# A gated linear attention and a gated scan on one core: the alpha copy, the first group's states, the first block and the last store in smaller pieces, and one block in the next turn

## The chip, the cores and the metric

The kernel runs on one core of one Trainium2 chip. The metric is the device time of one execution in microseconds (us). Engines are named TensorE (PE, with its weight loads PEld), VectorE (DVE), ScalarE (ACT), GpSimd (POOL) and SyncE (SP, here a queue that issues transfers).

## What is computed

```python
# B, H, S, D = 4, 8, 768, 48
for t in range(S):
    state = alpha[:, :, t, :, None] * state + einsum('bhd,bhe->bhde', k[:, :, t], v[:, :, t])
    y[:, :, t] = einsum('bhd,bhde->bhe', q[:, :, t], state)
x = y as (B, S, H * D)                       # 384 columns
val, gate = split(x @ w_in)                  # 512 columns each
h[t] = exp(A_log) * h[t - 1] + val[t]        # a scan over S, per column
out = (silu(gate) * h) @ w_out               # 384 columns
```

All arithmetic is in float32; the weights come as 64-bit numbers and are converted on the chip.

## The kernel before

**Tiling.** Each of the 4 sequences is cut into 3 groups of 256 steps, which gives 12 groups, m = 0 to 11. A group has G = 2 chunks of 128 steps and four half chunks of L = 64. The 8 heads lie in two halves of partitions (i = 0, 1), with four heads along the free axis in each.

**Attention of a group m.** Alpha, q and k are brought to a layout with the channels along partitions, either by products with the identity on TensorE and copies by ACT (`turned`, L675, `copy_turned`, L685; a pair of PSUM banks for each tensor; `alphas` and `straighten` do the whole of it) or by a transpose on VectorE (`turn`, L589, in all later groups). Then `scan_P` (L620) forms running products of alpha, `scan_V` (L629) the reversed scan that k is scaled by, with three small operations between the two scans (ratio, L634 or L636, ends, L638, lower, L640). `scaled_k` and `scaled_q` write Zk and Zq. `scores` (L709) multiplies them into two pairs of PSUM banks, one pair for each chunk; `masks` (L722) takes the causal part on VectorE and copies the rest (K, dS) by ACT. `values` and `carried` form the output y of the group, `states` (L769) the half chunks' contributions to the state, which `add_banks` or, for later sequences, `add_up` sum. `first_values`, `first_carried`, `first_states` and `first_join` (L816 to L852) do the same for group 0, with v in the tile `wide` and the summed states in `wide_S`. `join` puts y into xT with transfers.

**Projection of a group n.** `project(n, cc)` (L880), cc = 0 to 3, makes two products of 128 x 256 from three input blocks kk each, a scan over them on VectorE (hh, L894), a silu on ACT (sg, L899); the function that it returns multiplies the two into f (L901), on VectorE for n below 2, else on POOL. `output(n)` (L903) makes two products of 128 x 384 with w_out; ACT copies each out and SP stores it.

**Weights.** `low(i)` (L535, ACT) and `convert(i)` (L541, two operations of VectorE and an addition on POOL) make weight part i; parts 0 to 3 are w_in for cc = 0 to 3, parts 4 and 5 the halves of w_out. `project(0, cc)` needs part cc.

**Order.** The program is scheduled by hand: each engine works off its instructions in the order of the calls. What stands before the loop (L920 to L976) is group 0's attention. Turn n of the loop (L998) holds the projection of group n and the attention of group n + 1; turns 0 and 1 are written out singly, as they still convert weights and straighten groups 1 to 3 on TensorE. PSUM has four banks in a ring (tag "mm") and the fixed banks s0, s1, y0 and y1. `bank_pair("s")` takes the fixed pair. A transfer waits on its queue until the one eight before it has landed.

Of the kernel before, what the change touches and what calls it, by code (L numbers as in the profile page):

```python
# [345 lines left out]
def fast(  # L346
# [143 lines left out]
    def constants():  # L490
# [23 lines left out]
        for n, t in enumerate(Zqs):  # L514
            for i in range(2):
                rows = ds(64 * i, 64)
                nc.gpsimd.tensor_copy(out=t[rows, :, :, 0:D].rearrange("p u h d -> p (u h) d"),
                                      in_=ident[rows, None, ds(64 * i, D)].to_broadcast([64, 8 * G, D]))
            if n == 0:
                load_v(0, nc.gpsimd)  # L520
                nc.gpsimd.memset(tri, 1.0)
                nc.gpsimd.affine_select(out=tri, in_=tri, compare_op=ALU.is_ge, fill=0.0, base=0,
                                        channel_multiplier=-1, pattern=[[1, C]])
                for h in range(2):
                    nc.gpsimd.tensor_copy(out=mask[ds(L * h, L)], in_=tri[ds(L * h, L), ds(L * h, L)])

    def bits_of(i):
# [100 lines left out]

    def scan_V(m, P):  # L629
        al = als[m % 2]  # L630
        g = m % NG
        last = P[:, :, GC]
        if g:
            nc.vector.tensor_mul(ratio[:, m], last, ends[:, :, GC])  # L634
        else:
            nc.vector.tensor_scalar(out=ratio[:, m], in0=last, scalar1=1.0 / FIRST_PRODUCT, scalar2=None,  # L636
                                    op0=ALU.mult)
        nc.vector.reciprocal(ends[:, :, GC], last)  # L638
        if g < NG - 1:
            nc.vector.tensor_copy(out=lower[:, :, 0], in_=last)  # L640
        V = p1.tile([C, 4 * GP], FP32, tag="V", name="V")
        nc.vector.tensor_tensor_scan(out=V[:, ::-1], data0=al[:, 1:4 * GP + 1][:, ::-1],  # L642
                                     data1=ends.rearrange("p h t -> p (h t)")[:, ::-1],
                                     initial=0.0, op0=ALU.mult, op1=ALU.add)
        return by_place(V)

# [27 lines left out]

    def turned(m, name, part, t):  # L675
        raw = steps_of(name, m)
        tp = t.rearrange("p (j x) -> p j x", j=NJ // 2)
        for j in range(NJ // 2):
            for i in range(2):
                nc.tensor.matmul(tp[ds(64 * i, 64), j],  # L680
                                 raw[:, ds(i * ROW + (NJ // 2 * part + j) * D, 64)], ident,
                                 start=True, stop=True, skip_group_check=True)
        return tp.rearrange("p j (c h) -> p h c j", h=4)

    def copy_turned(to, part, tp):  # L685
        nc.scalar.activation(by_runs(to)[:, :, :, ds(NJ // 2 * part, NJ // 2)], tp, AF.Copy)  # L686

    def alphas(m, tag=None):
        to = by_place(als[m % 2])[:, :, 1:GP]
        for part, t in enumerate(bank_pair(tag)):  # L690
            copy_turned(to, part, turned(m, "a", part, t))

    def straighten(m, name):
        to = plain(name)
        for part, t in enumerate(bank_pair()):
            copy_turned(to, part, turned(m, name, part, t))
        return to
# [10 lines left out]

    def scores(m):  # L709
        Zk, Zq = Zks[m], Zqs[m % 2]  # L710
        scs[m] = [bank_pair("s"), bank_pair()]
        for c in range(G):
            for p in range(4):
# [55 lines left out]
    def states(m):  # L769
        first = (m % NG) * 2 * G  # L770
        st = [t[:, 0:G * 4 * D].rearrange("p (c j d) -> p c j d", c=G, j=4) for t in bank_pair("s")]
        n = [G, G - (first + 2 * G == NS)]
        for c in range(G):
            for p in range(4):
                for h in range(2):
                    if c < n[h]:
                        rows = ds(L * h, L)
                        for i in range(2):
                            nc.tensor.matmul(st[h][ds(64 * i, 64), c, p, :], (K0, dS[m % 2][1])[i][rows, c, p, :] if m < NG else Ks[i][rows, c, p, :],  # L779
                                             wide[rows, c, ds(2 * D * (4 * i + p), D)] if m == 0 else  # L780
                                             vs[m % NV][rows, c, 4 * i + p, 0:D],
                                             start=True, stop=True, skip_group_check=True)
# [3 lines left out]
        for h in range(2):  # L786
            nc.scalar.activation(parts[h][:, 0:n[h], :, 0:D], st[h][:, 0:n[h]], AF.Copy)  # L787

# [12 lines left out]
    def add_banks(m, st):  # L801
        for u in range(4):
# [3 lines left out]
            Ss[j] = sums[j % NB]  # L806
            nc.vector.tensor_add(Ss[j][:, :, 0:D], st[u % 2][:, u // 2], Ss[j - 1][:, :, 0:D])

# [21 lines left out]
    def first_carried(us):  # L830
        for u in us:
            for i in range(2):
                rows = ds(64 * i, D)
# [4 lines left out]
    def first_states(st):  # L838
        to = [t.rearrange("p (h d) -> p h d", d=D)[:, ::2, :] for t in wide_S]
        Ss[3] = sums[3]  # L840
        to.append(sums[3][:, :, 0:D])
        nc.scalar.activation(to[0], st[0][:, 0], AF.Copy)
        for u in range(1, 4):
            nc.vector.tensor_add(to[u], st[u % 2][:, u // 2], to[u - 1])

# [33 lines left out]

    def project(n, cc):  # L880
        if cc == 0:
# [6 lines left out]
        pv, pg = [t[:, 0:GC] for t in bank_pair()]  # L888
        for vg, pj in enumerate((pv, pg)):
            for kk in range(NK):  # L890
                nc.tensor.matmul(pj, w_ins[cc][:, kk, vg, :], xT[:, kk, :],  # L891
                                 start=(kk == 0), stop=(kk == NK - 1))
        hh = p2.tile([C, GC], FP32, tag=f"h{cc}", name="hh")
        nc.vector.tensor_tensor_scan(  # L894
            out=hh, data0=a_dec[:, cc:cc + 1].to_broadcast([C, GC]), data1=pv,
            initial=prev_h[cc][:, GC - 1:GC] if n % NG else 0.0, op0=ALU.mult, op1=ALU.add)
        prev_h[cc] = hh
        sg = p2.tile([C, GC], FP32, tag="sg", name="sg")
        nc.scalar.activation(sg, pg, AF.Silu)  # L899
        engine = nc.vector if n < 2 else nc.gpsimd  # L900
        return lambda: engine.tensor_mul(fs[n][cc], sg, hh)  # L901

    def output(n):  # L903
        b, g = divmod(n, NG)
        os = [t[:, 0:DM] for t in bank_pair()]
        def evict(c):
            o_sb = p2.tile([C, DM], FP32, tag="o_sb", name="o_sb")
            nc.scalar.activation(o_sb, os[c], AF.Copy)  # L908
            nc.sync.dma_start(out=out[b, ds(g * GC + c * C, C), :], in_=o_sb)

        for ccs in (range(NI - 1), range(NI - 1, NI)):
            for c in range(G):
# [3 lines left out]
                if ccs.stop == NI:  # L916
                    evict(c)

# [20 lines left out]
    keep_warm(3, 256)  # L939
    alphas(0, "s")  # L940
    tq = straighten(0, "q")
# [9 lines left out]
    P = scan_P(0)  # L951
    V = scan_V(0, P)
    half = turned(1, "k", 0, bank())
    for c in range(G):
        scaled_k(0, tk, V, c)
        scaled_q(0, tq, P, c)
    tk = plain("k")
    copy_turned(tk, 0, half)
    scores(0)
    masks(0)  # L960
    low(0)
    convert(0)
# [35 lines left out]
    for n in range(N):  # L998
        m = n + 1
        if n == 0:  # L1000
            f0 = project(n, 0)
            copy_turned(tk, 1, turned(1, "k", 1, bank()))
            tq = straighten(1, "q")
            V = scan_V(1, P)
            low(2)
            scaled_k(1, tk, V)
            convert(2)
            f1 = project(n, 1)
            low(3)
            scaled_q(1, tq, P)  # L1010
            f0()
            f1()
            alphas(2)
            tk = straighten(2, "k")
            load_raw("k", 3, nc.sync)
            convert(3)
            first(m)
            tq = straighten(2, "q")
            load_raw("q", 3, nc.sync)
            junk(1)  # L1020
            low(4)
            P = scan_P(2)
            f2 = project(n, 2)
            V = scan_V(2, P)
            values(m, True)
            st = states(m)
            add_banks(m, st)
            f3 = project(n, 3)
            third(m)
            load_v(3, nc.sync)  # L1030
            for c in range(G):
                scaled_k(2, tk, V, c)
                scaled_q(2, tq, P, c)
            f2()
            f3()
        elif n == 1:
            scores(m)
            alphas(3)
            load_raw("a", 4, nc.sync)
            convert(4)  # L1040
            masks(m)
            junk(2)
            low(5)
            values(m, True)
            st = states(m)
            P = scan_P(3)
            f0 = project(n, 0)
            add_banks(m, st)
            convert(5)
            f1 = project(n, 1)  # L1050
            f0()
            tk = plain("k")
            turn("k", tk)
            load_raw("k", 4, nc.sync)
            third(m)
            load_v(4, nc.sync)
            f1()
            junk(3)
            V = scan_V(3, P)
            f2 = project(n, 2)  # L1060
            scaled_k(3, tk, V)
            f2()
            output(0)
            f3 = project(n, 3)
            tq = plain("q")
            turn("q", tq)
            scaled_q(3, tq, P)
            f3()
        else:
            first(m)  # L1070
            if n > 1:
                load_raw("q", n + 2, nc.sync)
# [72 lines left out]
```

## Time and profile before

| | us |
|---|---|
| median of 3 runs (lowest, highest) | 288.7 (288.54, 290.04) |
| the profiled execution | 288.26 |
| its span on the core | 286.5 |
| first alpha product on TensorE | 4.57 |
| first P scan on VectorE, from and to | 8.11, 10.41 |
| first scores on TensorE | 14.57 |
| project(0, 0) on TensorE begins | 23.62 |
| project(1, 0) on TensorE begins | 54.05 |
| scores(3) on TensorE begin | 76.69 |
| last copy out on ACT, from and to | 280.17, 280.66 |
| last store landed | 284.33 |

The span is that of the program's instructions on the core. The time of the execution has 1.8 us around it. A row of a timeline has the start, the time taken, the engine, the line, the operation, the tiles (out<-in) with partitions x elements, and how many instructions are merged in it. On TensorE a float32 product counts as two instructions. A row's time includes the drain of the pipeline, so the next row can start before it ends. TensorE's granted clock was full over the span, apart from the tail. The alpha products at 4.57 still went at half the later pace until 5.87 (0.213 us for a pair of rows, then 0.110).

### The profile page before, as it was taken

What the parts mean: (1) busy time and instruction counts of PE and PEld (TensorE: products, weight loads), DVE (VectorE), ACT (ScalarE), POOL (GpSimd) and SP (SyncE); (2) the same over time, 40 slices, a digit from 0 to 9 for tenths busy, and PEclk for the clock granted to TensorE, in tenths of its full rate; (3) what the DMA queues carried; (4) which work ended last, traced back from release to release, by engine and by line L of the source; (5) the groups of instructions that cost most, each with busy time, mean ns of one, the idle gap of its engine ahead of it and who ended that gap; (6) DMA issues with size and microseconds to landing.
All of it is one profiled execution on the core that took longest, in us unless ns stands there. A gap on an engine that the chain in (4) does not pass through costs nothing.

```text
span 286.5 us, 9591 instructions
## 1 busy us (share of the span) xinstructions
PE 276.3 (96%) x4096; PEld 220.2 (77%) x4096; DVE 217.1 (76%) x276; ACT 110.5 (39%) x242; POOL 94.7 (33%) x108
## 2 busy tenths in 40 slices
PE   7889999999999999999999999999999999999991
PEld 6888888886688688788787787787786886886860
DVE  7888999996599499499499498597696795299310
ACT  3765672651335325324333343442451451431111
POOL 8125221420046155142154173142172172241220
PEclk9999999999999999999999999999999999999997
DMA  6999871715691981981972962964944901100101
GB/s 187 345 281 321 249 186 30 185 25 135 170 207 37 228 203 41 235 190 44 256 168 66 261 140 66 268 137 107 250 114 110 239 16 30 59 21 23 55 6 63
DMA packets 51524, 41.22 MB, mean 144 GB/s; under 512 B 27312, under 2 KB 49264, under 8 KB 51472
## 3 DMA queue, kind: packets, MB, share of 16 engines
q1 hardware_dynamic: 50256, 39.37, 52.9%
q8 instruction: 34, 0.56, 0.9%
q10 hardware_dynamic: 960, 0.59, 0.8%
q0 software_dynamic: 256, 0.56, 0.7%
q14 instruction: 18, 0.15, 0.2%
HBM read 32.54 MB, written 4.72 MB: 130 GB/s over the span
## 4 chain that ended last, share of the span: by engine, by line
PE 87%; DVE 7%; DMA 1%; ACT 1%; issue 1%; DVEq 0%; ACTq 0%
PE mm L891 44%; PE mm L914 22%; PE y L752 4%; PE s L779 4%; PE y L765 4%; PE s L718 3%; PE mm L718 3%; PE mm L680 2%; DVE P L625 2%; DVE V L642 2%; DMA raw_a<-in_alpha_dram 1%; PE s L680 1%; PE y L835 1%; DVE Zk L609 1%; PE y L827 1%
## 5 line engine op out<-in xcount | busy, mean ns | idle before, releaser
L891 PE MATMUL mm<-xT,w_in 128*128 128x256 f32 x576 | 133.9, 385 | 0.3 <-ACT xT L849 0.3
L891 PEld LDWEIGHTS mm<-xT,w_in 128*128 128x128 f32 x576 | 106.5, 190 | 17.2 <-issue 0.7
L914 PE MATMUL mm<-w_out,f 128*128 128x384 f32 x176 | 58.6, 486 | 0.0
L914 PEld LDWEIGHTS mm<-w_out,f 128*128 128x128 f32 x176 | 33.4, 190 | 21.0
L899 ACT ACTIVATE sg<-mm 128x256 f32<-128x256 f32 x48 | 18.5, 385 | 76.0 <-PE mm L891 75.8
L901 POOL TENSOR_TENSOR f<-sg,hh 128x256 f32<-128x256 f32 x40 | 30.6, 767 | 45.9 <-ACT sg L899 44.5
L799 POOL TENSOR_TENSOR sum<-sum,dS 128x192 f32<-128x192 f32 x30 | 30.0, 1001 | 19.9 <-ACT dS L787 18.4
L736 POOL TENSOR_TENSOR AK<-AK,mask 128x512 f32<-128x512 f32 x9 | 11.5, 1277 | 68.2 <-ACT AK L734 68.2
L894 DVE TENSOR_TENSOR_SCAN hh<-a_dec,hh,mm 128x256 f32<-128x256 f32 x32 | 23.0, 719 | 14.5 <-PE mm L891 12.3
L908 ACT ACTIVATE o_sb<-mm 128x384 f32<-128x384 f32 x24 | 11.8, 491 | 50.3 <-PE mm L914 50.3
L642 DVE TENSOR_TENSOR_SCAN V<-al,ends 128x1028 f32<-128x1028 f32 x12 | 30.6, 2548 | 0.1
L625 DVE TENSOR_TENSOR_SCAN P<-al,lower 128x1028 f32<-128x1028 f32 x12 | 28.6, 2380 | 2.1 <-ACT al L686 2.0
L733 DVE TENSOR_TENSOR A<-s,mask 128x256 f32<-128x256 f32 x9 | 3.8, 424 | 30.5 <-PE s L718 30.5
L590 DVE STREAM_TRANSPOSE k<-raw_k 128x1024 f32<-128x1024 f32 x9 | 18.3, 2030 | 0.0
L590 DVE STREAM_TRANSPOSE q<-raw_q 128x1024 f32<-128x1024 f32 x9 | 18.2, 2017 | 0.0
L600 DVE TENSOR_TENSOR Zq<-q,P 128x1024 f32<-128x1024 f32 (+1 forms) x14 | 16.3, 1166 | 0.3
L590 DVE STREAM_TRANSPOSE al<-raw_a 128x1024 f32<-128x1024 f32 x8 | 16.3, 2043 | 0.0
L552 POOL TENSOR_TENSOR w_in<-w_in,wr 128x768 int32<-128x768 int32 x4 | 9.1, 2286 | 21.7 <-DVE w_in L550 21.7
L752 PEld LDWEIGHTS y<-AK,v 64*64 64x64 f32 x352 | 12.2, 134 | 3.8 <-issue 3.3
L752 PE MATMUL y<-AK,v 64*64 64x64 f32 x352 | 14.7, 221 | 0.2 <-DVE lower L624 0.2
L609 DVE TENSOR_TENSOR Zk<-k,V 128x1024 f32<-128x1024 f32 (+1 forms) x14 | 14.7, 1050 | 0.2
L752 PE MATMUL y<-A,v 64*64 64x64 f32 x352 | 14.7, 221 | 0.0
(129 smaller groups left out, 362.8 us busy)
## 6 DMA issues: line engine op xcount, KB each, us to landing
out_dram<-o_sb SPq DMA_DIRECT2D x24, 192.0 KB, 3.5
v<-in_v_dram SPq DMA_DIRECT2D x22, 192.0 KB, 3.5
raw_k<-in_k_dram SPq DMA_DIRECT2D x18, 184.0 KB, 4.0
raw_q<-in_q_dram SPq DMA_DIRECT2D x18, 184.0 KB, 3.9
raw_k<-in_k_dram SPq DMA_DIRECT2D x18, 176.0 KB, 4.0
raw_q<-in_q_dram SPq DMA_DIRECT2D x18, 176.0 KB, 4.4
wbits<-in_moe_w_in_dram SPq DMA_DIRECT2D x4, 768.0 KB, 7.9
raw_a<-in_alpha_dram SPq DMA_DIRECT2D x16, 184.0 KB, 4.7
```

Of the source, the lines that this page charges most:

```text
L590: nc.vector.transpose(out=by_runs(to).rearrange("p h c j -> p h j c"), in_=raws[name][:, 0:4 * ROW].rearrange("p (h j d) -> p h j d", h=4, ...
L609: nc.vector.tensor_mul(Zks[m][:, ds(c0, n)].rearrange("p c h t -> p h c t"), t[:, :, at].rearrange("p h (c t) -> p h c t", t=C), V[:, :, 1 ...
L625: nc.vector.tensor_tensor_scan(out=P, data0=al[:, 0:4 * GP], data1=lower.rearrange("p h t -> p (h t)"), initial=0.0, op0=ALU.mult, op1=ALU ...
L642: nc.vector.tensor_tensor_scan(out=V[:, ::-1], data0=al[:, 1:4 * GP + 1][:, ::-1], data1=ends.rearrange("p h t -> p (h t)")[:, ::-1], init ...
L718: nc.tensor.matmul(scs[m][c][i][ds(L * h, L), ds(p * (L + D), L + D)], Zk[rows, c, p, ds(h * L, L)], Zq[rows, u, p], start=True, stop=True ...
L752: nc.tensor.matmul(ys[m][i][ds(64 * s, 64), e, ds(c * C + h * L, L)], v_sb[rows, c, 4 * i + p, :], As[i][rows, c, p, :], start=across and ...
L799: nc.gpsimd.tensor_add(Ss[j][:, :, 0:D], Ss[j - 1][:, :, 0:D], part)
L891: nc.tensor.matmul(pj, w_ins[cc][:, kk, vg, :], xT[:, kk, :], start=(kk == 0), stop=(kk == NK - 1))
L894: nc.vector.tensor_tensor_scan(out=hh, data0=a_dec[:, cc:cc + 1].to_broadcast([C, GC]), data1=pv, initial=prev_h[cc][:, GC - 1:GC] if n % ...
L899: nc.scalar.activation(sg, pg, AF.Silu)
L901: return lambda: engine.tensor_mul(fs[n][cc], sg, hh)
L914: nc.tensor.matmul(os[c], fs[n][cc][:, ds(c * C, C)], w_outs[cc // 2][:, cc % 2, :], start=(cc == 0), stop=(cc == NI - 1))
```

## The change

- Alpha of group 0 goes through four banks (s0, s1, y1, y0) in quarters, with four copies of 256 columns by ACT, where there were two of 512. v of group 0 is loaded by POOL after both Zq tiles and the mask have been made, instead of between the two Zq tiles.
- `scan_V` keeps only what V needs ahead of V. The ratio of a sequence's first group and `lower` come after it (`after_V`), for group 0 after the masks.
- The second half of straighten(1, k) moves from turn 0 to between the two chunks of scores(0).
- `states(0)` uses two pairs of banks, one for each chunk.
- `first_carried` finishes y[0] before y[1], and `project(0, 0)` goes through the input blocks kk in the outer loop.
- In turns 0 and 1 project(0, 3) moves from turn 0 to turn 1, the conversions 2 to 5 and the products f stand elsewhere, and q of group 3 is loaded in the other layout and straightened by TensorE and ACT (`straighten(3, "q")`) instead of turned by VectorE.
- The last store of the program is made in two halves, copied out by ACT and VectorE and stored from ACT's and SP's queues.

```diff
-            if n == 0:
-                load_v(0, nc.gpsimd)
+            if n:
                 nc.gpsimd.memset(tri, 1.0)
...
+                load_v(0, nc.gpsimd)
...
+    def after_V(m, P):
         last = P[:, :, GC]
+        if m % NG == 0:
+            nc.vector.tensor_scalar(out=ratio[:, m], in0=last, scalar1=1.0 / FIRST_PRODUCT, scalar2=None,
+                                    op0=ALU.mult)
+        if m % NG < NG - 1:
+            nc.vector.tensor_copy(out=lower[:, :, 0], in_=last)
...
+    def turn_over(m, name, to, tags=(None, None)):
+        size = NJ // len(tags)
+        for n, tag in enumerate(tags):
+            js = range(size * n, size * (n + 1))
+            copy_turned(to, js, turned(m, name, js, bank(tag)))
...
+        pair = bank_pair("s")
+        pairs = [pair, bank_pair() if m == 0 else pair]
...
     def first_carried(us):
-        for u in us:
-            for i in range(2):
+        for i in range(2):
+            for u in us:
...
+        order = [(vg, kk) for vg in range(2) for kk in range(NK)]
+        if n == 0 and cc == 0:
+            order.sort(key=lambda x: x[1])
...
-                    evict(c)
+                    if n < N - 1 or c == 0:
+                        evict(c)
+                    else:
+                        evict(c, 0, DM // 2, nc.scalar, nc.scalar)
+                        evict(c, DM // 2, DM // 2, nc.vector, nc.sync)
...
-    alphas(0, "s")
+    alphas(0, ("s0", "s1", "y1", "y0"))
...
-    scores(0)
+    copy_turned(tk, halves[0], part)
+    scores(0, [0])
+    copy_turned(tk, halves[1], turned(1, "k", halves[1], bank()))
+    scores(0, [1])
     masks(0)
+    after_V(0, P)
```

Turns 0 and 1 as they stand after the change:

```python
        if n == 0:
            f0 = project(n, 0)
            tq = straighten(1, "q")
            load_steps("q", 3, [nc.sync])
            V = scan_V(1, P)
            low(2)
            f1 = project(n, 1)
            scaled_k(1, tk, V)
            scaled_q(1, tq, P)
            alphas(2)
            tk = straighten(2, "k")
            load_raw("k", 3, nc.sync)
            convert(2)
            first(m)
            tq = straighten(2, "q")
            junk(1)
            low(3)
            P = scan_P(2)
            f0()
            f1()
            values(m, True)
            st = states(m)
            add_banks(m, st)
            h2, f2 = project(n, 2, True)
            V = scan_V(2, P)
            third(m)
            load_v(3, nc.sync)
            for c in range(G):
                scaled_k(2, tk, V, c)
                scaled_q(2, tq, P, c)
                if c == 0:
                    h2()
        elif n == 1:
            scores(m)
            alphas(3)
            load_raw("a", 4, nc.sync)
            low(4)
            masks(m)
            convert(3)
            f2()
            junk(2)
            values(m, True)
            st = states(m)
            add_banks(m, st)
            g0 = project(n, 0)
            P = scan_P(3)
            low(5)
            f3 = project(0, 3)
            convert(4)
            f3()
            g0()
            convert(5)
            g1 = project(n, 1)
            third(m)
            load_v(4, nc.sync)
            tk = plain("k")
            turn("k", tk)
            load_raw("k", 4, nc.sync)
            g1()
            tq = straighten(3, "q")
            load_raw("q", 4, nc.sync)
            junk(3)
            V = scan_V(3, P)
            output(0)
            g2 = project(n, 2)
            scaled_k(3, tk, V)
            scaled_q(3, tq, P)
            g2()
            project(n, 3)()
```

With `late`, `project` returns the scan hh and the product f as two functions, to be called where they are wanted (`h2`, `f2`).

## The prediction

> **What bounds the kernel now.** I read the busy times first, then the chain of waits in order of time, then TensorE's own waits and VectorE's timeline for the first 55 us.
>
> ```profile
> PE 276.3 (96%) x4096; PEld 220.2 (77%) x4096; DVE 217.1 (76%) x276; ACT 110.5 (39%) x242; POOL 94.7 (33%) x108
> ...
> PE 87%; DVE 7%; DMA 1%; ACT 1%; issue 1%; DVEq 0%; ACTq 0%
> ```
>
> TensorE is busy for 276.3 of 286.5 us. The second line is the chain that ended last: TensorE, with VectorE's 7% in the first 53 us. By stretches TensorE is busy all of 60.0 to 260.0 us, so only the start, the first two turns and the tail can give anything, and any matmul added there is paid in full.
>
> TensorE's waits (total, times, longest):
>
> ```profile
> PE s L718 <- DVE Zq L600: 1.0, 1, 1.0
> PE y L835 <- ACT wide_S L842: 0.4, 1, 0.4
> PE mm L891 <- ACT xT L849: 0.3, 1, 0.3
> PE mm L718 <- ACT k L686: 0.2, 1, 0.2
> PE y L752 <- DVE lower L624: 0.2, 1, 0.2
> ```
>
> Four lie before 23.62 us. After that TensorE idles 0.2 us until the tail. VectorE is nearly as full there (11.47 of the 12.38 us from 23.62, 13.45 of the 14.00 from 40.00). Its timeline around the end of turn 0, with TensorE's rows for the scores of group 2 last:
>
> ```profile
> 38.24 2.71 DVE L625 TENSOR_TENSOR_SCAN P<-al,lower 128x1028 f32<-128x1028 f32 x1
> 40.94 0.69 DVE L894 TENSOR_TENSOR_SCAN hh<-a_dec,mm 128x256 f32<-128x256 f32 x1
> 41.54 0.14 DVE L634 TENSOR_TENSOR ratio<-P,ends 128x4 f32<-128x4 f32 x1
> 41.72 0.18 DVE L638 RECIPROCAL ends<-P 128x4 f32<-128x4 f32 x1
> 41.94 2.30 DVE L642 TENSOR_TENSOR_SCAN V<-al,ends 128x1028 f32<-128x1028 f32 x1
> 44.15 1.58 DVE L807 TENSOR_TENSOR sum<-s,sum 128x192 f32<-128x192 f32 x4
> 45.65 0.68 DVE L894 TENSOR_TENSOR_SCAN hh<-a_dec,mm 128x256 f32<-128x256 f32 x1
> 46.24 0.67 DVE L609 TENSOR_TENSOR Zk<-k,V 128x512 f32<-128x512 f32 x1
> 46.82 0.69 DVE L600 TENSOR_TENSOR Zq<-q,P 128x512 f32<-128x512 f32 x1
> 47.42 0.69 DVE L609 TENSOR_TENSOR Zk<-k,V 128x512 f32<-128x512 f32 x1
> 48.03 0.69 DVE L600 TENSOR_TENSOR Zq<-q,P 128x512 f32<-128x512 f32 x1
> ```
>
> ```profile
> 47.91 0.95 PE L718 MATMUL s<-Zq,Zk 48*64 48x112 f32 x32
> 48.77 1.00 PE L718 MATMUL mm<-Zq,Zk 48*64 48x112 f32 x32
> ```
>
> The second Zq ends at 48.72 and its scores start at 48.77: the two engines arrive together. VectorE's chain from masks(1) to this Zq has no slack; TensorE's 2.79 us of project(0, 3), at 43.67, is what covers it.
>
> **The start.** All times are on the clock of the profile of before.
> - *Alpha in quarters.* The last alpha matmul ends at 7.24 either way. The last copy runs 7.36 to 8.07 for 512 columns; 256 columns take 0.38 (xT, L849), and since alpha's copies run slower than others (0.67 to 0.71 against 0.60) I take 0.42. The first three quarters end by about 7.3, before the last is ready. Scan P starts at 7.82, not 8.11: -0.29 (bounds -0.33 and 0).
> - *After_V behind the masks.* P to V is 10.41 to 10.72; with the reciprocal alone (0.17 and two hand-offs of 0.03) 0.23: -0.08. Scores c 0 start at 14.20, not 14.57.
> - *Second half of k(1) between the scores.* 16 instructions, 0.92 us (26.55 to 27.47), now at 15.08 to 16.00. Scores c 1, which ACT's k copy held until 15.77, use other banks and start at 16.00: +0.23, and so for masks, first_values and states.
> - *Four banks of states.* The states' last issue moves from 19.26 to 19.49. Chunk 0 of them is ready at about 19.20 (18.20 + 0.23 + half of 1.03 + 0.25 of drain), its copy ends at 19.53, first_carried starts at 19.6 instead of 19.86: -0.26.
> - *Input rows first.* The 60 products to the end of first_carried take 2.97 to issue (19.86 to 22.83), so TensorE is free at 22.57. y[0] is done twelve products (0.64) before y[1]; its xT copy (0.39) ends near 22.6. project(0, 0) starts at 22.75, taking the present 0.15 from copy to matmul, instead of 23.62, and lasts 2.79 instead of 2.93.
> It ends at 25.54, not 26.55, with the half of k already done, so straighten(1, q) starts at 25.54 instead of 27.47: **-1.93** (bounds -1.2, if the hand-offs eat half of it, and -2.4, if all early waits vanish).
>
> **Turn 0, TensorE,** from 25.54 with the present durations: q(1) 1.85, project(0, 1) 2.79, alphas(2) 1.80, k(2) 1.85, which gives 33.83; scores(1) 1.69, so chunk 0 is readable near 34.9 and chunk 1 near 35.75; q(2) 1.90, values and states 1.54, project(0, 2) 2.79, third(1) 1.45. TensorE wants scores(2) at 43.2.
>
> **Turn 0, VectorE.** Convert(2) is over near 33.3; VectorE waits for scores(1). Masks end, and P starts, near 36.5. Then, start to start: P 2.22 (2.71 above includes waiting for POOL, whose w_in add ran 36.97 to 38.79; convert(2)'s add now ends earlier), f0 and f1 0.67, four sums 1.50, ratio and reciprocal 0.40, V 2.21, Zk 0.58, Zq 0.69: 8.27. The scores' c 0 starts near 44.8: TensorE idles 1.6. Then h2 0.60, Zk 0.60, Zq 0.69: c 1 starts near 46.6, while c 0 was through by 45.66: another 0.95. **New wait 2.5** (bounds 1.6 and 3.0: all hand-offs at zero; P again 0.5 longer). project(0, 3) had hidden it; taking convert(3) off VectorE helps nothing there, since VectorE idles before masks(1) anyway.
>
> **Turn 1.** Scores(2) end at 47.5 instead of 49.70; alphas(3) 1.92, values(2) 0.6: 50.0. Low(4) (0.89) now stands on ACT ahead of the copies of K and dS. Alpha's second copy ends near 50.25, low(4) near 51.05, K and dS of chunk 0 near 51.5. States end near 52.5 and project(1, 0) starts there, instead of 54.05. Values and states take about 3.05 against 2.43: **+0.62** (bounds 0 and 1.0). Convert(3) and f2 are covered by this.
> Straighten(3, q) replaces VectorE's transpose (2.02): 32 more matmul rows at 0.057, **+1.85** (bounds 1.80 and 1.95), paid in full, as TensorE is full behind it. ACT's two copies (0.60) and the loads hide: SP's two transfers of q(3) (1.2) go out in its gap between a(3), issued by 33.14, and k(3), 35.86; q(4) under output. The moved project(0, 3) is neutral by itself.
>
> **The tail.** The last ACT copy shrinks from 0.49 to 0.33 (192 columns, L842); VectorE's half (0.38) runs beside it. The last two stores now land 0.46 apart, so half a store is worth 0.23, but there is one more store: **-0.2** (bounds -0.5 and +0.1).
>
> **Sum.** -1.93 + 2.5 + 0.62 + 1.85 - 0.2 = +2.84, say +2.9: 288.26 (the profiled execution, span 286.5) becomes 291.2. The median of the runs shown is 288.7, so **291.6**. All low bounds give +0.5, all high ones +4.9; they are independent, so +1.8 to +4.0 for this case alone.
>
> **Rivals.**
> 1. *VectorE keeps up*: no new wait at scores(2) and none at states(2). Then -1.93 + 1.85 - 0.2 = -0.3, 288.4, not slower. It decides if VectorE's 10.2 us from P to the last Zq shrink to under 7.7. Against it: each duration above is a row of an uncontended instruction; for it, only that chains of this length have been put together from rows. Chance 0.11.
> 2. *The start gives nothing*: copies in quarters and the longer way through k(1) cost as much as they save, so only the half of k (0.92) is gained: +1.0 more, 292.6. For it: scores c 1 do start later. Against: 0.35 and 0.28 of the waits have a direct cause that goes. Chance 0.07.
> 3. *v(0) comes late.* Its two POOL issues (1.98 together at 3.09) now stand behind the second Zq pair (1.69) and the mask (1.13): they go out near 5.9 to 7.9 and, by the present 6.5 and 7.1, land by 12.5 and 14.5, before first_values at 16.9 and 17.9. But scan P starts at 7.8. An add on POOL that met scan P at 22.59 took 3.68 us instead of 1.82. If the second issue were held until V ends at 12.6, it would land near 20.6 and everything behind shift by 2.7: 294.3. Chance 0.06.
> The Trainium skill (SBUF — State Buffer, SBUF: two separate sides) warns of this: descriptors of a POOL transfer cannot be written while VectorE holds the pair of ports that both share. The same page (Who interferes with whom) has an instruction with two SBUF inputs contend only with POOL instructions that read SBUF. By the first rule rival 3 would hold, by the second not; the add at 22.59 reads SBUF, so it agrees with both, and no row of before settles it.
>
> **How the numbers follow.** The forecast has 0.76, the rivals 0.11, 0.07, 0.06. A measurement here tells about 0.5% (1.4 us) from no change. Faster needs 287.3: only the low edge of rival 1, 0.03. Within: the rest of rival 1 and the forecast's low edge, 0.12. Slower 0.85. Range 289.8 to 293.3: the forecast's own 290.5 to 292.7, widened towards rivals 1 and 2.
>
> **What would show it.** TensorE waiting about 1.6 and 0.9 us for Zq at scores(2), where it waited 0.0; a wait over 1 us of the states(2) for ACT's K; project(0, 0) starting near 22.75; 32 more L680-type matmuls in turn 1; both transfers of v(0) landed by 15. If TensorE does not wait at scores(2), the forecast is wrong by that wait; if project(0, 0) starts after 23.4, the first term is.

## The result, and the profile after

The changed kernel takes 299.28 us in the median of 4 runs (297.34 to 305.1), the kernel before 288.99 beside it (4 runs): a ratio of 1.034, 95% interval 1.028 to 1.040. It is slower, as forecast, but by 10.3 us where 2.9 were forecast, and outside the range. The profiled execution of the changed kernel is its slowest (305.1), with the lowest mean clock (0.965); the ratios here and below leave out runs over 1.5% above the fastest of their kernel, which the medians keep.

The page of the changed kernel: its first lines, the granted clock and the chain.

```profile
span 303.3 us, 9672 instructions
...
PE 285.9 (94%) x4128; PEld 228.4 (75%) x4128; DVE 214.8 (71%) x276; ACT 111.4 (37%) x246; POOL 99.5 (33%) x108
...
PEclk9995899599999999999999999999999999999997
...
PE 86%; DVE 7%; DMA 2%; issue 1%; ACT 1%; POOL 1%; DVEq 0%; ACTq 0%
```

TensorE has 32 more rows (4128; a float32 product is two rows) but 9.6 us more busy time, and the busy time hides why: the digits of PEclk fall to 5 twice. Two windows (time, TensorE, weight loads, VectorE, ACT, POOL, granted clock, DMA share, GB/s) show it, first of the kernel before, then of the changed kernel:

```profile
23.00:30.00 7.00, 6.72 (x73) 5.49 (x68) 6.15 (x7) 4.68 (x11) 3.26 (x1) 1.00 1.00 359
...
50.00:60.00 10.00, 9.84 (x178) 8.40 (x175) 9.53 (x15) 4.92 (x11) 4.34 (x5) 1.00 0.63 146
```

```profile
23.00:30.00 7.00, 7.00 (x88) 6.34 (x85) 2.03 (x1) 2.54 (x6) 3.63 (x1) 0.50 1.03 373
...
50.00:60.00 10.00, 7.66 (x168) 6.76 (x161) 6.87 (x13) 2.95 (x7) 3.97 (x5) 0.67 0.32 72
```

By the trace's clock records TensorE ran at half speed from 22.66 to 32.90 and from 53.38 to 60.20; before, only in the tail. The products of project(0, 0) then follow each other every 0.43 us, where they took 0.215 before; all of this counts as busy, so the loss stands in no list of waits. What it cost can be read by comparing the same rows with a profile in which the clock was full there: 4.6 us for the first stretch (count 706 to 1150 of TensorE's rows, 18.1 us against 13.5 in e3_fill without its stop) and 2.9 us for the second (8.2 against 5.3 in e1_tail, without waits). The waits of TensorE in the changed kernel:

```profile
PE s L724 <- DVE Zq L600: 2.3, 2, 1.6
PE y L846 <- issue: 1.9, 1, 1.9
...
PE y L771 <- issue: 1.0, 1, 1.0
PE mm L724 <- DVE Zq L600: 0.8, 1, 0.8
PE s L788 <- ACT K L736: 0.8, 1, 0.8
```

The first line holds the old wait at scores(0) and a new one of 1.6 at scores(2); the fourth line is scores(2), second chunk; the fifth is states(2). These three were forecast. The two "issue" lines, in which TensorE stands still for nothing that the profile shows, were not. VectorE's rows at scores(2) show the forecast chain, with nothing idle between P and the last Zq:

```profile
43.54 2.29 DVE L625 TENSOR_TENSOR_SCAN P<-al,lower 128x1028 f32<-128x1028 f32 x1
...
50.72 0.69 DVE L609 TENSOR_TENSOR Zk<-k,V 128x512 f32<-128x512 f32 x1
51.33 0.68 DVE L600 TENSOR_TENSOR Zq<-q,P 128x512 f32<-128x512 f32 x1
51.93 0.68 DVE L909 TENSOR_TENSOR_SCAN hh<-a_dec,mm 128x256 f32<-128x256 f32 x1
52.53 0.66 DVE L609 TENSOR_TENSOR Zk<-k,V 128x512 f32<-128x512 f32 x1
53.11 0.68 DVE L600 TENSOR_TENSOR Zq<-q,P 128x512 f32<-128x512 f32 x1
```

The tail of the changed kernel:

```profile
293.65 0.49 ACT L929 ACTIVATE o_sb<-mm 128x384 f32<-128x384 f32 x1 [4.07 <-PE mm L937]
294.17 4.73 SPq L932 DMA_DIRECT2D out_dram<-o_sb  x2
294.30 0.33 ACT L929 ACTIVATE o_sb<-mm 128x192 f32<-128x192 f32 x1 [0.15 <-PE mm L937]
...
298.18 0.36 DVE L931 COPY o_sb<-mm 128x192 f32<-128x192 f32 x1 [9.52 <-DMA out_dram<-o_sb]
```

VectorE's half does not run beside ACT's: it starts 3.9 us later, released by a store. The tile o_sb has two buffers; this is the third use in a row, so it waits until the first of the last stores has landed. From TensorE's end (294.26) to the end of the span are 9.0 us, where 6.4 were (280.13 to 286.54).

### The profile page after: what moved, and what is told of

Its sections match the earlier page's. It is cut to its first block, busy times and chain, and to the rows that moved or that the text cites. A ratio compares the mean times of both kernels' runs of the same rounds, so it can differ in the third digit from the quotient of the medians.

```text
span 303.3 us, 9672 instructions
## 1 busy us (share of the span) xinstructions
PE 285.9 (94%) x4128; PEld 228.4 (75%) x4128; DVE 214.8 (71%) x276; ACT 111.4 (37%) x246; POOL 99.5 (33%) x108
## 4 chain that ended last, share of the span: by engine, by line
PE 86%; DVE 7%; DMA 2%; issue 1%; ACT 1%; POOL 1%; DVEq 0%; ACTq 0%
PE mm L904 43%; PE mm L937 20%; PE y L771 3%; PE mm L724 3%; PE y L758 3%; PE s L724 3%; PE s L788 3%; PE mm L684 3%; DVE V L644 2%; DVE P L625 1%; DMA out_dram<-o_sb 1%; PE y L846 1%; DMA raw_a<-in_alpha_dram 1%; PE y L838 1%; DVE Zk L609 1%
## 5 line engine op out<-in xcount | busy, mean ns | idle before, releaser
L904 PE MATMUL mm<-xT,w_in 128*128 128x256 f32 x576 | 135.8, 390 | 0.0
L904 PEld LDWEIGHTS mm<-xT,w_in 128*128 128x128 f32 x576 | 108.5, 193 | 17.1 <-issue 0.2
L919 POOL TENSOR_TENSOR f<-sg,hh 128x256 f32<-128x256 f32 x40 | 35.6, 892 | 41.8 <-ACT sg L917 38.5
L929 ACT ACTIVATE o_sb<-mm 128x384 f32<-128x384 f32 (+1 forms) x24 | 11.6, 485 | 49.9 <-PE mm L937 49.9
L909 DVE TENSOR_TENSOR_SCAN hh<-a_dec,mm 128x256 f32<-128x256 f32 x16 | 10.5, 658 | 10.7 <-PE mm L904 10.7
L590 DVE STREAM_TRANSPOSE q<-raw_q 128x1024 f32<-128x1024 f32 x8 | 16.2, 2019 | 0.0
L771 PEld LDWEIGHTS y<-Zq,sum 48*64 48x64 f32 x656 | 11.9, 134 | 4.8 <-POOL sum L810 2.7
L771 PE MATMUL y<-Zq,sum 48*64 48x64 f32 x656 | 14.4, 222 | 1.0 <-issue 1.0
L724 PEld LDWEIGHTS s<-Zq,Zk 48*64 48x64 f32 x384 | 9.4, 132 | 7.7 <-PE mm L937 4.4
L600 DVE TENSOR_TENSOR Zq<-q,P 128x1024 f32<-128x1024 f32 (+1 forms) x14 | 15.0, 1070 | 0.3
```

The costliest lines, as they stand in the source:

```text
L590: nc.vector.transpose(out=by_runs(to).rearrange("p h c j -> p h j c"), in_=raws[name][:, 0:4 * ROW].rearrange("p (h j d) -> p h j d", h=4, ...
L600: nc.vector.tensor_mul(Zqs[m % 2][:, ds(u0, n), :, D:].rearrange("p u h t -> p h u t"), t[:, :, at].rearrange("p h (u t) -> p h u t", t=L) ...
L724: nc.tensor.matmul(scs[m][c][i][ds(L * h, L), ds(p * (L + D), L + D)], Zk[rows, c, p, ds(h * L, L)], Zq[rows, u, p], start=True, stop=True ...
L771: nc.tensor.matmul(ys[m][i][ds(64 * s, 64), e, ds(u * L, L)], Ss[j][rows, p, :], Zqs[m % 2][rows, u, p, D:], start=False, stop=True, skip_ ...
L904: nc.tensor.matmul((pv, pg)[vg], w_ins[cc][:, kk, vg, :], xT[:, kk, :], start=(kk == 0), stop=(kk == NK - 1))
L909: nc.vector.tensor_tensor_scan(out=hh, data0=a_dec[:, cc:cc + 1].to_broadcast([C, GC]), data1=pv, initial=prev_h[cc][:, GC - 1:GC] if n % ...
```

## The experiments

Each ran beside the kernel before. The last column is the median with the clock's loss taken out: each run's time less its span times (1 - its mean granted clock). This is rough: idle time at half clock counts as lost, and so does the tail behind TensorE's last product, where the clock falls in every profile (0.3 to 2.6 us of the subtraction). Differences under about 2 us in that column show nothing by themselves.

| kernel | median us (runs) | ratio to before, 95% | mean clock of the runs | clock out, us |
|---|---|---|---|---|
| before (beside them) | 288.2 to 289.0 | | 0.985 to 1.000 | 287.0 to 287.4 |
| after | 299.28 (4) | 1.034, 1.028 to 1.040 | 0.965 to 0.990 | 294.0 |
| e1_tail | 296.27 (4) | 1.026, 1.019 to 1.033 | 0.978 to 0.995 | 291.8 |
| e2_start | 289.73 (9) | 1.004, 1.000 to 1.008 | 0.981 to 0.999 | 288.1 |
| e3_fill | 297.10 (4) | 1.028, 1.024 to 1.033 | 0.991 to 0.994 | 294.6 |
| e4_turns | 296.64 (4) | 1.023, 1.015 to 1.031 | 0.977 to 0.995 | 292.8 |
| e5_gate | 292.24 (6) | 1.013, 1.008 to 1.018 | 0.976 to 0.998 | 287.7 |
| e6_last | 288.42 (12) | 1.001, 0.998 to 1.004 | 0.992 to 0.999 | 287.3 |
| e7_best | 289.92 (12) | 1.005, 1.002 to 1.008 | 0.980 to 0.997 | 288.3 |
| e8_turned | 295.29 (4) | 1.020, 1.013 to 1.028 | 0.983 to 0.996 | 292.2 |
| e9_back | 296.85 (4) | 1.030, 1.023 to 1.037 | 0.983 to 0.997 | 294.6 |
| e10_pad | 297.92 (6) | 1.028, 1.023 to 1.034 | 0.980 to 0.986 | 292.5 |
| e11_low | 295.41 (4) | 1.023, 1.016 to 1.030 | 0.983 to 0.996 | 292.7 |
| e12_room | 292.66 (4) | 1.014, 1.010 to 1.019 | 0.994 to 0.999 | 291.9 |

### The tail: e1_tail and e6_last

e1_tail is the changed kernel with a tile of its own for VectorE's half; e6_last is the kernel before with its last store made in these halves.

```diff
-            o_sb = p2.tile([C, DM], FP32, tag="o_sb", name="o_sb")
+            if copy is nc.scalar:
+                o_sb = p2.tile([C, DM], FP32, tag="o_sb", name="o_sb")
+            else:
+                o_sb = p1.tile([C, DM // 2], FP32, tag="o_half", name="o_half")
```

> The changed kernel, with a tile of its own for VectorE's half of the last store, so that this half no longer waits until an earlier store has landed and frees one of the two o_sb tiles. Theory (that wait is the tail's loss: VectorE's copy began 3.9 us after the last matmul): 2.5 to 3 us faster than the changed kernel, about 296.5 us by its median of 299.28, and VectorE's copy within 0.3 us of the last matmul. Rival (the tail costs nothing, all is lost earlier): within 0.5 us of 299.3.

> Before, with nothing changed but the last store: two halves, copied by ACT and VectorE and stored from two queues, VectorE's half in a tile of its own. Theory (the price of 0.2 us in the prediction was right once the wait for the tile is gone): 0 to 0.5 us below before. Rival (halves and a second queue cost more to finish than they save): 0.2 to 1 us above before.

The tail of e1_tail:

```profile
288.46 0.33 ACT L932 ACTIVATE o_sb<-mm 128x192 f32<-128x192 f32 x1 [0.15 <-PE mm L940]
288.82 0.37 ACTq L935 DMA_DIRECT2D out_dram<-o_sb  x1
288.82 0.36 DVE L934 COPY o_half<-mm 128x192 f32<-128x192 f32 x1 [6.00 <-ACT o_sb L932]
```

VectorE's half now starts at 288.82 instead of 3.9 us behind ACT's, and 5.7 us pass from TensorE's end (288.42) to the span's (294.16). The median is 3.0 lower than that of the changed kernel, 2.2 with the clock out. From TensorE's end to the span's end the two profiles differ by 3.3. So the buffer wait cost 2 to 3 us. Even here VectorE begins only when ACT's half has ended. In e6_last the split store makes no difference that can be measured (ratio 1.001, 0.998 to 1.004). Its profile also has a fall of the clock that none of the changed parts made: at half from 16.60 to 20.01, in a start that is that of before.

### The start and the turns apart: e2_start and e4_turns

e2_start has the change ahead of the loop and the turns and tail of before; e4_turns has the new turns 0 and 1, and start and tail of before. In e4_turns the second half of straighten(1, k) stands in turn 0 again; in e2_start turns 0 and 1 are those of before without that half:

```diff
             f0 = project(n, 0)
-            copy_turned(tk, 1, turned(1, "k", 1, bank()))
             tq = straighten(1, "q")
```

> Only the start of the change (alpha in quarters, four banks of states, first block by rows, half of k between the scores, v later): turns 0 and 1 and the last store as before. Theory (the turns and the tail hold the loss): 287 to 289 us, that is 1 to 2 us below before, with the half of k gained. Rival (the start itself loses: TensorE stands still 1.9 us in first_carried, with no wait that the profile shows, and its clock then falls to half for 10 us): 292 us or more, with the clock at half between 22 and 33 us.

> Only the new order of turns 0 and 1 (project(0, 3) in turn 1, straighten(3, q) on TensorE, conversions moved); start and last store as before. Theory (wait for Zq at scores(2) 2.5 us, wait for K at states(2) 0.6, extra products 1.85, and 3.4 us of the clock at half): 295 to 298 us. Rival (the clock falls only in the start, and the new wait is all): 292 to 294.5 us. Rival 1 of the prediction (VectorE keeps up): below 291 us.

The start alone does not gain: 289.73, ratio 1.004 (1.000 to 1.008). Two of its nine runs have a clock of 0.985 and 0.981. The waits of TensorE in e2_start hold two stops that the kernel before does not have:

```profile
PE mm L684 <- PE mm L904: 0.9, 1, 0.9
...
PE y L846 <- issue: 0.2, 1, 0.2
```

The first is put down to the matmul ahead of it on the same engine, which is no cause; it is a stop of the "issue" kind with another name. Scores(1) start at 35.91 against 35.75 before: 0.16 later in spite of 1.1 us of stops, so the rest of the start saves about 0.95. That is hardly more than the half of straighten(1, k) that it no longer holds (0.92). Scores(0) start 0.28 earlier, but from there to first_carried TensorE takes 5.58 us with the new start (e2_start and the changed kernel) and 5.29 with the old one, so the products put between the scores eat this. The start also differs from run to run: over the 14 profiles the first scan P begins between 7.03 and 8.59, nearly always the later the later the clock came up (4.28 to 9.92). Only profiles with like clocks can be compared there: 7.90 in e2_start (clock up at 5.98) against 8.11 before (6.04), 8.23 in e12_room (7.01) against 8.41 in e11_low (7.05), so the quarters of alpha save about 0.2.

The turns alone cost 8.4 us in the median (296.64 against 288.21 beside it) and 5.5 with the clock out. In the profiled execution TensorE ends at 288.48, 8.35 us later than before. Of it 2.34 are the two waits at scores(2) (45.23 to 46.78, 47.78 to 48.56), 0.9 states(2), 0.7 a stop at 177.1, 1.85 the 32 rows of products; they make 5.8. From 47.79 to 54.62 the clock was at half, which cost 2.8 by the same rows in e11_low, where it was full.

### Filling the wait: e3_fill

The changed kernel with six products ahead of scores(2) whose results nothing reads.

```diff
         elif n == 1:
+            t = bank("s1")
+            for _ in range(6):
+                nc.tensor.matmul(t[:, 0:256], wide_S[0][:, 0:C], wide_S[0][:, 0:256], start=True, stop=True,
+                                 skip_group_check=True)
             scores(m)
```

> The changed kernel, with six products of 128 x 256 on the tile wide_S, whose results nobody reads, on TensorE ahead of scores(2), so that it is busy while VectorE makes Zq. Theory (TensorE's clock falls to half after the stretch of waiting at scores(2), 7 us at half in the profile): the wait itself stays, the clock stays full after it, about 3 us faster than the changed kernel, 296 us. Rival (the clock falls for another reason, such as the earlier fall in first_carried): no change, 299 us, or slower by the products.

With the wait filled, no run of four has a mean clock under 0.991, and the profiled one, at 0.991, has no fall ahead of the tail. The changed kernel is under 0.983 in all but one of six executions (0.965 to 0.982, and 0.990), and e4_turns at 0.987 or less in three of four. The time with the clock out is no lower (294.6), since the fill takes the place of the wait. That the fill keeps the clock is suggested and not shown: the sample is small, the start of e3_fill lost no clock either, which the fill behind it can't explain, and e1_tail and e11_low had the same two waits in their profiles without a fall there. A fall stood behind these waits in the profiles of the changed kernel, e4_turns and e8_turned.

### Undoing the turns in parts: e8_turned, e9_back and e11_low

All three start from e4_turns. e8_turned turns q of group 3 on VectorE again (with its load as before, not shown):

```diff
-            tq = straighten(3, "q")
...
+            tq = plain("q")
+            turn("q", tq)
```

e9_back puts project(0, 3) back in turn 0, with low(3) and convert(3) ahead of masks(1):

```diff
+            convert(3)
             first(m)
...
+            h3, f3 = project(n, 3, True)
             third(m)
...
-                if c == 0:
-                    h2()
+                (h2, h3)[c]()
...
-            convert(3)
...
-            f3 = project(0, 3)
```

e11_low moves low(4) behind the states of group 2:

```diff
-            low(4)
             masks(m)
...
             P = scan_P(3)
+            low(4)
             low(5)
```

> e4_turns with q of group 3 turned by VectorE again, as before, instead of straightened by TensorE and ACT. Theory (32 more rows of products are paid in full): 1.85 us below e4_turns of the same clock, about 294.8 against 296.6 by medians, TensorE's waits at scores(2) and states(2) as there. Rival (VectorE's transpose of 2.02 us stops TensorE in turn 1 instead): within 0.5 us of e4_turns.

> e4_turns with project(0, 3) in turn 0 again, ahead of third(1), and conversion 3 in VectorE's gap before masks(1). Theory (project(0, 3) is what covers VectorE's chain to Zq): the wait at scores(2) falls from 2.3 us to under 0.7, the clock does not fall there, 291 to 293 us. Rival (the wait belongs to VectorE's order and stays): the wait over 1.5 us, 295 us or more.

> The new order of turns 0 and 1 alone, but low(4) stands behind the states of group 2 and scan P of group 3 instead of ahead of the masks. Theory, that the wait of states(2) for ACT's K is low(4) ahead of the copies: the wait of 0.9 us falls under 0.3 and the time loses 0.6 to 1.2 us, 295.4 to 296.0 (291.9 after the granted clock is taken out, against 292.8). Rival, that the copies of K and dS would be late anyway, since ACT's alpha copies or the masked scores set them: the wait stays over 0.6, 296.6.

e8_turned falls by 1.35 us in the median and by 0.6 with the clock out, where 1.85 us of products went; with four runs each neither is clear of the scatter. TensorE's waits show where the rest went:

```profile
PE s L724 <- DVE Zq L600: 2.5, 2, 1.6
PE mm L935 <- POOL w_out L552: 1.5, 1, 1.5
PE mm L684 <- issue: 1.4, 1, 1.4
```

The second line is new: output(0), now earlier, waits 1.5 for the conversion of w_out on POOL, which the products had covered.

e9_back is a miss: 296.85, no faster than e4_turns. The waits at scores(2) are still 0.75 and 0.79. VectorE's rows of e9_back ahead of scan P show why:

```profile
37.65 2.46 DVE L550 SCALAR_TENSOR_TENSOR w_in<-wbits,w_in 128x768 uint32<-128x768 uint32 x1
40.03 0.41 DVE L734 TENSOR_TENSOR A<-s,mask 128x256 f32<-128x256 f32 x1
```

The second operation of convert(3) took 2.46 us, where that of convert(2) took 0.96 at 36.18, and held the masks until 40.03, so P began at 41.35. So the covering products alone do not restore the order of before; the place of the conversions belongs to it. TensorE ends 8.35 later than before with a full clock: 0.75 + 0.79 at scores(2), 1.19 at states(2), 1.61 for w_out at output(0), 1.66 + 0.48 of stops and 1.85 for the products are 8.3. That they meet is in part luck, as first_carried starts 0.71 earlier here; counted from there, 0.7 us stay open.

In e11_low the wait of states(2) falls to 0.43 (0.9 in e4_turns, where the clock was at half, and 1.2 in e1_tail, e3_fill and e9_back, where it was full), not below 0.3. With low(4) gone, K's copy follows ACT's second alpha copy at once:

```profile
51.94 0.68 ACT L689 ACTIVATE al<-mm 128x512 f32<-128x512 f32 x1 [0.20 <-PE mm L684]
52.50 0.34 ACT L736 ACTIVATE K<-s 128x192 f32<-128x192 f32 x1
```

So low(4) made about two thirds of it at full clock, and the alpha copies the rest. The median falls by 1.2, but with the clock out it does not change (292.7 against 292.8), so the gain itself is not shown.

### Where TensorE stops: e5_gate, e7_best, e10_pad and e12_room

Count TensorE's rows in the trace (matmuls, weight loads and those of its sequencer) from 0, in the order in which they start. Over all 14 profiles, every stop of over 0.3 us marked "issue" (and that put down to the product ahead in e2_start) ends with number 705, 961, 5569 or 6849: 705 plus a multiple of 256. The kernel before and e6_last have none. The profile also has a DMA queue for instructions, for the whole span of the changed kernel (packets, MB, share of the engines):

```profile
q8 instruction: 34, 0.56, 0.9%
```

That is 34 packets of 16 KB for some 8300 rows of TensorE, about one for 256 of them. Taking the packets and the blocks in order, at each such stop over 0.5 us TensorE went on 1.3 to 1.6 us after the block's packet had ended, and in none of the profiles did it enter a block less than 1.2 us after. The Trainium skill (Runtime: NRT & Kernel Launch, Instruction fetch mechanics) says that instructions come in blocks of 16 KiB or 256 instructions over the engine's own DMA queue, while the block before is worked off, and that a crossing is mostly hidden. The blocks agree with the packets; at these stops the crossing was not hidden.

e5_gate is e2_start with the second half of w_in and k and q of group 2 loaded later; e7_best is e5_gate with e6_last's tail.

```diff
-    load_w(1, nc.sync)
-    for name in "kq":
-        load_steps(name, 2, [nc.sync])
...
     first_states(states(0))
...
+    nc.vector.memset(wbits[1][:, 0, :, 0:1, 0], 0)
+    load_w(1, nc.sync)
+    for name in "kq":
+        load_steps(name, 2, [nc.sync])
```

> e2_start with the second half of w_in, k(2) and q(2) loaded only after first_states: a small write of VectorE into their tile, behind first_states, holds the transfers back. Theory (TensorE's stops near 20 and 27 us, at the 705th and 961st of its profiled instructions, that is 256 apart, are waits for its next block of instructions, whose fetch stands behind data when the transfers are saturated): the stop near 20 us vanishes, project(0, 0) starts before 23.3 us, 287 to 288 us, 1 to 2 us below e2_start. Rival (the stops have nothing to do with the load of transfers): stops as in e2_start, the same time within 0.5 us or slower by later weights.

> e5_gate with the last store of e6_last: the parts of the change that should pay, without the turns. Theory: 286.5 to 287.8 us, below before and below e5_gate by 0 to 0.5. Rival (the start gains nothing even without the stops): within 0.5 us of before.

Both miss: e5_gate takes 292.24, e7_best 289.92. The stop at count 961 is gone from e5_gate's profile, but one of 1.3 us at count 705 (19.58 to 20.87) is there, and the clock was at half from 21.77 to 28.59, so TensorE reached count 961 only after 30 us and the missing stop there proves nothing. e7_best's profile has the same stop, 1.8 us long, and 10.24 us at half clock behind it. The fetch for 705 (18.49 to 19.44) follows a stretch that other loads fill, which were not held (DMA share 1.11 from 15 to 18 us).

Two runs settle what the stops are. e10_pad is e2_start with its three first products of 128x256 made into 27 of 16x16, which shifts all later instructions by 96 places (the clock came up at 9.92 in its profile, where it was 5.98 in that of e2_start):

```diff
-            nc.tensor.matmul(t[:, 0:w], wide_S[0][:, 0:C], wide_S[0][:, 0:w], start=True, stop=True,
+            nc.tensor.matmul(t[0:w, 0:w], wide_S[0][:, 0:w], wide_S[0][:, 0:w], start=True, stop=True,
...
-    keep_warm(3, 256)
+    keep_warm(27, 16)
```

> The start of the change alone (as in the run of that part), with 27 products of 16x16 as the first work of TensorE instead of 3 of 128x256, so that all later instructions stand 96 places later in TensorE's stream. Theory, that TensorE stands still where its instructions cross from one block of 256 to the next before the block has been fetched: the stalls stay at the counts 705, 961, 1217 of this stream, which are other instructions now. So no stall of 0.9 us ahead of straighten(1, q), whose first product starts at 26.4 to 27.0 instead of 27.58; at most 0.6 us somewhere in first_carried. The time goes to 288.3 to 289.3. Rival, that the stalls belong to those rows (a wait that the trace does not name): 0.4 us in first_carried and 0.9 ahead of straighten(1, q) as before, 289.7.

The stops stayed at the counts 705 and 961, which are other rows now (in states(0) and in the middle of first_carried), so they belong to the count and not to the work. The size was a miss: 297.92 instead of 288.3 to 289.3. The row of TensorE in e10_pad:

```profile
27.50 2.24 PE L846 MATMUL y<-Zq,wide_S 48*64 48x64 f32 x35 [3.79 <-issue]
```

TensorE now reaches count 961 at 23.5, and the block still arrives when it did: fetched 25.19 to 26.11, against 25.10 to 25.99 in e2_start. All six runs have a clock of 0.980 to 0.986; in the profiled one it was at half from 26.99 to 33.81 again.

e12_room is e10_pad with the loads held until scan P of group 1 has ended:

```diff
     P = scan_P(1)
+    nc.vector.memset(wbits[1][:, 0, :, 0:1, 0], 0)
+    load_w(1, nc.sync)
+    for name in "kq":
+        load_steps(name, 2, [nc.sync])
     first_carried((1,))
```

> The padded start (27 small products first), and the second half of w_in, k and q of group 2 and, behind them in SP's queue, w_out, v(2) and alpha(3) go out only when scan P of group 1 has ended on VectorE (near 25), so that the transfer engines have room from 18 to 25. Theory, that the block at count 961 came late (fetched at 25.19 to 26.11, 4.7 us after TensorE entered the block before) since its fetch stands behind the loads: it is fetched by 23.0, and the stall of 4.0 us ahead of count 961 falls under 1.0. The time itself may not gain, since the held loads come 5 us later and TensorE may then wait for k(2) and for w_in near 34: 289 to 294. Rival, that the fetches keep a pace of their own (some 6 us apart, whatever else moves): fetched at 24.7 or later, and the stall stays at 3.5 to 4.5.

The same stretch from 20.5 to 24.9 us in the DMA view, with the instructions' queue where it has packets: first e10_pad, then e12_room.

```profile
DMA packets 698, 1.32 MB, mean 301 GB/s; under 512 B 31, under 2 KB 113, under 8 KB 698
...
q1 hardware_dynamic: 698, 1.32, 89.1%
```

```profile
DMA packets 2, 0.02 MB, mean 6 GB/s; under 512 B 0, under 2 KB 0, under 8 KB 0
...
q8 instruction: 1, 0.02, 1.9%
```

In e10_pad the loads fill the engines and no instruction packet comes through; in e12_room it comes 1.0 us after TensorE entered the block before. The blocks at count 961, and for comparison those of before (from the traces, us):

| kernel | block before entered | fetched | TensorE goes on | row gap there |
|---|---|---|---|---|
| before | 20.64 | 24.69 to 25.78 | 27.47 | 0.10 |
| e2_start | 20.52 | 25.10 to 25.99 | 27.58 | 0.98 |
| e10_pad | 20.49 | 25.19 to 26.11 | 27.50 | 4.00 |
| e12_room | 20.35 | 21.39 to 22.72 | 24.35 | 0.99 |

TensorE's waits in e12_room have what is left of the stop:

```profile
PE y L846 <- issue: 0.8, 1, 0.8
```

So at count 961 the fetch stands behind the loads, and TensorE stops if it is through its block first. The row gap of e10_pad falls to a quarter, no run of e12_room has a clock under 0.994 (e10_pad: 0.980 to 0.986), and the time falls by 5.3 us with the same instructions on TensorE. Why the fetches are late at 5569 and 6849, in the middle of the program, was not tested. The kernel before has no such stop: it reached count 961 at 27.47, when the block had been there for 1.7 us.

## Why the prediction was right in direction and wrong in size

Three steps failed: the start's gain, the tail's "runs beside it", and the clock and the supply of instructions, which the sum left at nothing. All three went the same way, so the direction held and the range did not.

- *The new wait at scores(2), +2.5*: right. 1.55 and 0.78 in the changed kernel and in e4_turns. Rival 1 (VectorE keeps up) is refuted by the same rows.
- *States(2) behind low(4), +0.62*: right in kind, too small. 1.2 in e1_tail and e3_fill; 0.8 in the changed kernel's profile, where the clock was down. e11_low shows that 0.43 of it come from the alpha copies.
- *Straighten(3, q), +1.85*: the 32 rows are there, behind a full TensorE. That they are paid in full was not isolated: e8_turned saved 0.6 with the clock out and waited 1.5 for w_out instead. The sum of the profiled execution below closes with the full 1.85.
- *The start, -1.93*: too large. The term's step "TensorE is free at 22.57" failed. The last of the 60 products starts at 23.12 in the profile of before, not at 22.83, so they take 3.26 and not 2.97. In e2_start first_carried starts at 19.87, not 19.6 (19.63 in the changed kernel's profile), its last product at 23.66, with one stop, and project(0, 0) at 23.81, not 22.75. About 0.95 is saved and then eaten by stops of 1.1. Rival 2 (only the half of k is gained) gave this 0.92, and in part for its reason: the 0.29 us that the way through k(1) adds. The stops that eat it were in no rival.
- *Rival 3, v(0) late*: refuted. POOL issued at 6.02 and 7.10 and the transfers landed at 11.87 and 14.60, before the 15 that was named. The second issue took 0.90 us as before, though scan P began 0.34 us ahead of its end; that is too short an overlap to decide between the two rules named there.
- *The tail, -0.2*: wrong in sign. "VectorE's half (0.38) runs beside it" overlooked that the third o_sb in a row waits for a store: +2.6 from TensorE's end to the span's end. e6_last has no change that could be measured, which the -0.2 fits.

With the measured sizes the forecast's own terms give -0.95 + 2.34 + 1.2 + 1.85 + 2.6 = +7.0. The other 3.3 of the 10.3 were in no term: TensorE's stops at instruction blocks and the clock, which the forecast took as that of before, full over the span. In the profiled execution, the slowest, both are larger and the sum closes: -1.2 for the start (0.23 up to first_carried, and 0.96 from there to scores(1) by e2_start's rows without their stops), 2.3 at scores(2), 0.8 at states(2), 1.85 for the products, 2.6 for the tail, 2.9 for the stops that end at 21.95 and 183.64, and 7.5 for the two stretches at half clock make 16.75, where the span grew by 16.76. What makes the clock fall stays open. The three parts of the change add up to more when each is taken alone (8.4 + 1.5 + 3.0 = 12.9 by medians); they are medians of four to nine runs that scatter by 4 to 8 us, with the falls of the clock in them.

No version tried beats the kernel before; e6_last equals it.

## What to carry to other kernels

Before a split store or copy is booked as running beside another, count the buffers of its tile: the third use of two buffers waits for a landed transfer. A wait added on TensorE costs its length, and in some executions a stretch at half clock stood behind it (2.8 us for 6.83 us at half in e4_turns), so look at the granted clock by stretch and not at busy time. Where short products run through 256 rows in 3 to 6 us (e10_pad, e2_start) while loads fill the DMA engines, moving TensorE earlier can gain nothing, because it then waits for its own instructions; compare the packets of the instructions' queue with the stops marked "issue", and leave the loads a gap there.

## What the runs showed of the hardware that was not expected

- 96 tiny instructions at the start of TensorE's stream cost 8.2 us in the median (297.92 against 289.73; by the ratios to before 1.028 against 1.004). In the profile 3.8 us of it are one stop and 2.7 the clock at half behind it, by the same rows in e12_room.
- All falls of the clock in the middle of a profile last a multiple of 3.41 us: 10.24 in the changed kernel and e7_best, 6.82 or 6.83 in the changed kernel, e1_tail, e4_turns, e5_gate and e10_pad, 3.41 in e8_turned and e6_last. The cost, by the same rows at full clock, is 4.6 us for 10.24 and 2.7 to 3.0 for 6.83. The Trainium skill (TensorE: Matmul & The Clock Gate, Part 1) has a free-running window of 3413 ns after whose idleness the clock halves. The lengths agree with the window, and e10_pad's fall at 26.99, 3.3 us after its stop began, with the rule. In e1_tail the clock fell at 21.9 with no standstill over 1.5 us ahead of it, among short products, so here less than an idle window was enough. The same waits at scores(2) had a fall behind them in some profiles and none in others, and e6_last's fell in the start of before. What decides whether it falls in a given execution stays open.
